# Another order for the beginning of a fused attention and feed-forward kernel: loads, norms and weight conversion

## The chip, the cores and the metric

The kernel runs on one core of one Trainium2 chip. The metric is the device time of one execution in microseconds (us).

Names used below: PE is TensorE, ACT ScalarE, DVE VectorE, POOL GpSimd, SPq the queue of SyncE that issues the loads and stores. A "values product" is PE's product of one pair's exponentials with its v (line L501 in the profiles). "Half clock" is a granted PE clock of 0.50 in the profile, as a share of full speed.

## The reference

```python
q, k, v: (8, 12, 448, 64) float32            # batch, heads, sequence, head size
q_n, k_n = rmsnorm(q) * g_q, rmsnorm(k) * g_k
attn = softmax(q_n @ k_n.T / 8) ; x = attn @ v   # then (B, H, S, D) -> (3584, 768)
xn = rmsnorm(x) * rms_g
out = (silu(xn @ w_gate) * (xn @ w_val)) @ w_out # weights are float64
```

The weights come as float64; the kernel converts them to float32 itself.

## The kernel before: what the change touches

Attention goes in 48 groups of two heads ("pairs", counted from 0). In iteration `g` PE computes the scores of pair `g`, transposes pair `g + 1` and multiplies pair `g - 1` with its values. The program fixes the order of instructions on each engine by itself; `pe(...)` emits PE's work and whatever other engines' work is due after it.

The norm of a pair is a chain over four engines: squares on ACT, sums on DVE, a power and a product on POOL, then PE's transposes, and copies to `qkT` by ACT and DVE:

```python
def squares(g, i):                       # i = 0: q, 1: k
    nc.scalar.activation(sq, st["qk", g][:, i], ACT.Square)
    after(1, reduce)                     # DVE, sums -> ms
    ...                                  # then POOL: rms_qk (power -0.5), norm_q -> qn
```

The conversion of weights is a pipeline that moves by one turn per `convert()`. Every engine has a part of it:

```python
def convert():
    ...
    if 0 <= n - 4 < len(pieces):         # POOL: add the two halves, block n - 4 is done
        ...
        nc.gpsimd.tensor_tensor(data(key).bitcast(I32), top, lo, ALU.add)
    if 0 <= n - 3 < len(pieces):         # DVE: join, three instructions
        st["cv", n - 3] = join(*st.pop(("cv", n - 3)))
    if 0 <= n - 2 < len(pieces):         # ACT: split, two instructions
        st["cv", n - 2] = split(st.pop(("raw", n - 2)))
    if n < len(pieces):                  # SPq: load of block n, into one of 6 buffers
        st["raw", n] = load_raw(pieces[n][1])
    if 0 <= n - 6 < len(pieces):         # SPq: store of block n - 6
        keep(pieces[n - 6][0])
```

The beginning:

```python
squares(0, 0)
pe(idle)
squares(0, 1)
pe(lambda: turn(0, 1))
convert(); convert()
bound()                                  # gains, and a flag from three one-row instructions
squares(1, 0); squares(1, 1)
pe(lambda: turn(0, 0))
convert()
for g in range(NG + 1):
    load_pair(g + 2)
    if g <= NPAIR:                       # NPAIR = 6
        pe(lambda: score(g, (0, 1)))     # 4 products, and 4 exponentials on ACT
        squares(g + 2, 0); squares(g + 2, 1)
        if g == 0:
            pe(lambda: score(g, (2, 3)))
        convert()
        pe(lambda: turn(g + 1, 0)); pe(lambda: turn(g + 1, 1))
        if g:
            pe(lambda: values(g - 1))
        load_v(g + 2)
        convert()
        if g:
            pe(lambda: sums(g - 1)); pe(lambda: score(g, (2, 3)))
        convert()
        continue
    ...                                  # later groups, with the feed-forward part between
```

## Time and profile before

| | before |
|---|---|
| median, 3 runs | 1637.91 us (1637.1 to 1639.52) |
| profiled span | 1636.9 us |
| PE busy | 1615.2 us, 99% |
| PE's waits, first 60 us | 12.5 us |
| PE's waits, rest | 3.0 us |
| first values product starts | 25.40 us |

A timeline line reads: start, duration, engine, source line, operation, tiles written and read, shapes, number of instructions merged; in brackets the idle time ahead of it and what ended it. Where such a line merges several pipelined products its duration contains small waits, so a "busy" PE is not PE at its peak. The lines themselves stand in the prediction.

### The profile page before, as it was taken

What the parts mean: (1) busy time and instruction counts of PE and PEld (TensorE: products, weight loads), DVE (VectorE), ACT (ScalarE), POOL (GpSimd) and SP (SyncE); (2) the same over time, 40 slices, a digit from 0 to 9 for tenths busy, and PEclk for the clock granted to TensorE, in tenths of its full rate; (3) what the DMA queues carried; (4) which work ended last, traced back from release to release, by engine and by line L of the source; (5) the groups of instructions that cost most, each with busy time, mean ns of one, the idle gap of its engine ahead of it and who ended that gap; (6) DMA issues with size and microseconds to landing.
All of it is one profiled execution on the core that took longest, in us unless ns stands there. A gap on an engine that the chain in (4) does not pass through costs nothing.

```text
span 1636.9 us, 21470 instructions
## 1 busy us (share of the span) xinstructions
PE 1615.2 (99%) x7376; PEld 1142.1 (70%) x7376; DVE 862.6 (53%) x1371; ACT 499.8 (31%) x975; POOL 631.3 (39%) x569
## 2 busy tenths in 40 slices
PE   6999999999999999999999999999999999999998
PEld 3444445678855888568875688758876587969984
DVE  6988998366542476426562354624555234433431
ACT  6756563233222332223223222322232123100110
POOL 6777777334423343334433333344343322100000
PEclk9999999999999999999999999999999999999999
DMA  7757674454613866665544655466454464557652
GB/s 195 227 158 204 183 228 128 141 185 142 211 51 117 254 203 222 204 196 162 154 139 120 196 154 159 119 204 192 146 148 124 151 192 114 146 179 241 174 150 65
DMA packets 246443, 273.28 MB, mean 167 GB/s; under 512 B 66356, under 2 KB 243252, under 8 KB 246324
## 3 DMA queue, kind: packets, MB, share of 16 engines
q1 hardware_dynamic: 246004, 271.80, 55.8%
q8 instruction: 61, 1.00, 0.3%
q14 instruction: 58, 0.48, 0.1%
q10 hardware_dynamic: 320, 0.00, 0.0%
HBM read 232.40 MB, written 39.32 MB: 166 GB/s over the span
## 4 chain that ended last, share of the span: by engine, by line
PE 92%; DVE 4%; DMA 2%; ACT 1%; SPq 0%; POOL 0%; issue 0%; DVEq 0%; ACTq 0%; POOLq 0%
PE ff L793 41%; PE ff L987 18%; PE sc L476 9%; PE av L501 8%; PE ff L888 7%; PE den L512 3%; PE ff L1018 2%; PE tr L461 2%; DVE top L646 1%; DVE top L644 1%; DVE top L645 1%; DVE rd L520 1%; DMA qk<-in_k_dram 1%; ACT e L480 1%; DMA raw<-in_moe_w_out_dram 0%; DMA raw<-in_moe_w_gate_dram 0%
## 5 line engine op out<-in xcount | busy, mean ns | idle before, releaser
L793 PE MATMUL ff<-x,w 128*128 128x224 f32 x2016 | 405.7, 353 | 0.0
L793 PEld LDWEIGHTS ff<-x,w 128*128 128x128 f32 x2016 | 378.5, 190 | 12.0 <-issue 6.6
L793 PE MATMUL ff<-xs,w 128*128 128x224 f32 x1512 | 308.0, 353 | 0.0
L793 PEld LDWEIGHTS ff<-xs,w 128*128 128x128 f32 x1512 | 283.4, 190 | 5.3 <-issue 5.3
L480 ACT ACTIVATE e<-sc,rs 112x448 f32<-112x448 f32 x384 | 212.0, 635 | 194.4 <-PE sc L476 189.3
L486 POOL TENSOR_TENSOR es<-e 112x448 f32<-112x448 f32 x82 | 95.1, 1181 | 455.9 <-ACT e L480 455.9
L490 POOL TENSOR_TENSOR es<-es,e 112x448 f32<-112x448 f32 x164 | 187.2, 1152 | 85.3 <-ACT e L480 78.8
L520 DVE RECIPROCAL rd<-rd 128x448 f32<-128x448 f32 x41 | 121.1, 2952 | 143.2 <-ACT rd L519 143.2
L987 PE MATMUL ff<-w,h 128*128 128x384 f32 x576 | 191.1, 487 | 0.0
L476 PE MATMUL sc<-qkT 64*112 64x448 f32 x768 | 179.0, 571 | 5.1 <-ACT qkT L464 5.1
L987 PEld LDWEIGHTS ff<-w,h 128*128 128x128 f32 x576 | 108.1, 190 | 75.5 <-issue 4.0
L501 PE MATMUL av<-e,vt 112*64 112x448 f32 x768 | 154.9, 545 | 0.0
L444 POOL TENSOR_TENSOR rs<-ms,mhalf 112x16 f32<-112x16 f32 (+1 forms) x50 | 143.4, 2867 | 4.2
L476 PEld LDWEIGHTS sc<-qkT 64*112 64x112 f32 x768 | 69.4, 174 | 98.0 <-issue 70.6
L501 PEld LDWEIGHTS av<-e,vt 112*64 112x64 f32 x768 | 50.8, 136 | 95.3 <-issue 75.2
L1018 PE MATMUL ff<-x,w 128*128 128x448 f32 x288 | 112.0, 542 | 0.0
L888 PE MATMUL ff<-w,h 128*128 128x384 f32 x336 | 111.0, 488 | 0.0
L987 PE MATMUL ff<-w,so 128*128 128x384 f32 x324 | 108.6, 488 | 2.0 <-DVE y L948 2.0
L805 DVE TENSOR_TENSOR cc<-ff,u 128x448 f32<-128x448 f32 x84 | 52.4, 624 | 90.4 <-PE ff L793 90.0
L888 PEld LDWEIGHTS ff<-w,h 128*128 128x128 f32 x336 | 62.8, 190 | 43.7 <-issue 2.7
L987 PEld LDWEIGHTS ff<-w,so 128*128 128x128 f32 x324 | 60.5, 190 | 44.7 <-DVE y L948 3.9
L1018 PEld LDWEIGHTS ff<-x,w 128*128 128x128 f32 x288 | 53.3, 190 | 50.8 <-issue 48.8
(86 smaller groups left out, 1470.5 us busy)
## 6 DMA issues: line engine op xcount, KB each, us to landing
w<-kept SPq DMA_DIRECT2D x552, 192.0 KB, 3.3
w<-kept_o SPq DMA_DIRECT2D x318, 192.0 KB, 3.0
kept<-w SPq DMA_DIRECT2D x96, 192.0 KB, 3.8
qk<-in_q_dram SPq DMA_DIRECT2D x48, 224.0 KB, 3.4
qk<-in_k_dram SPq DMA_DIRECT2D x96, 112.0 KB, 3.9
vt<-in_v_dram SPq DMA_DIRECT2D x48, 224.0 KB, 2.8
raw<-in_moe_w_gate_dram SPq DMA_DIRECT2D x24, 384.0 KB, 4.4
raw<-in_moe_w_val_dram SPq DMA_DIRECT2D x24, 384.0 KB, 4.7
```

The lines of the kernel that those rows point to most:

```text
L444: nc.gpsimd.tensor_tensor(st["rs", g][:, cols], ms, mhalf[0:P, cols], ALU.pow)
L476: nc.tensor.matmul(ps[0:P, 0:S], lhsT=qkT[r, 1, c * P:(c + 1) * P], rhs=qkT[r, 0, :], start=True, stop=True)
L480: nc.scalar.activation(e, ps[0:P, 0:S], ACT.Exp, scale=rs[:, n:n + 1])
L486: nc.gpsimd.tensor_tensor(es, st["e", g, 0, j], st["e", g, 1, j], ALU.add)
L490: nc.gpsimd.tensor_tensor(es, es, st["e", g, c, j], ALU.add)
L501: nc.tensor.matmul(av[j * D:(j + 1) * D, 0:S], lhsT=vt[:, j, c, :], rhs=st["e", g, c, j], start=(c == 0), stop=(c == NT - 1))
L520: nc.vector.reciprocal(rd, rd)
L793: nc.tensor.matmul(bank[:, w * HT:(w + 1) * HT], lhsT=wt[:, c * 128:(c + 1) * 128], rhs=x[:, c, :], start=onto is None and w == c == 0, st ...
L805: nc.vector.tensor_tensor(add[name], ps[:, 0:S], add[other], ALU.add)
L888: nc.tensor.matmul(ps, lhsT=st["h", b, fc][:, i * 128:(i + 1) * 128], rhs=data(("wo", b, *block_of(n, fc))), start=(fc == 0), stop=(fc == ...
L987: nc.tensor.matmul(ps, lhsT=a, rhs=data(("wo", b, name, c)), start=first and c == 0, stop=c == NFP - 1, skip_group_check=True)
L1018: nc.tensor.matmul(bank[w][:, 0:S], lhsT=data(key)[:, c * 128:(c + 1) * 128], rhs=st["x", 0, half][:, c, :], start=half == c == 0, stop=ha ...
```

## The change

The intent: PE idles and runs cold in the first 25 us because the third pair's q and k are loaded behind weights, and weight conversion and a flag stand in front of the work that PE needs. So load and square that pair first, convert weights later (the same number of turns by the end of the third group), compute the flag later, and keep PE warm with products of the identity until data come.

```diff
+    load_pair(2)
     for g in range(2):
         load_v(g)
...
     squares(0, 0)
+    warm(9)
     pe(idle)
     squares(0, 1)
     pe(lambda: turn(0, 1))
-    convert()
-    convert()
-    bound()
+    gains()
     squares(1, 0)
     squares(1, 1)
+    warm(3)
     pe(lambda: turn(0, 0))
-    convert()
+    squares(2, 0)
+    squares(2, 1)
     for g in range(NG + 1):
         b, hp = divmod(g, NPAIR)
-        load_pair(g + 2)
+        if g:
+            load_pair(g + 2)
+        if g == 0:
+            pe(lambda: score(0, (0, 1)))
+            pe(lambda: score(0, (2, 3)))
+            for i in range(2):
+                pe(lambda: turn(1, i))
+            load_v(2)
+            for _ in range(4):
+                convert()
+            load_rows()
+            continue
         if g <= NPAIR:
...
             convert()
+            if g <= 2:
+                convert()
+            if g == 2:
+                bound()
             continue
```

`warm(n)` issues n products of the 128x128 identity with itself into a bank that nobody reads. `gains()` and `load_rows()` are parts of what stood in `bound()` and ahead of it.

More of the change, by code (lines that the diff above doesn't have):

```diff
@@ L1099, in safe_scores, with gains, load_rows, bound @@
         nc.scalar.dma_start(out=gk[rows, :], in_=g_k.rearrange("(p o) -> p o", o=1))
+    load_pair(2)
     for g in range(2):
         load_v(g)
+    gqk = const.tile([128, 1], F32, name="gqk")
     rg = const.tile([128, NDC], F32, name="rg")
-    nc.sync.dma_start(out=rg, in_=moe_rms_g.rearrange("(c p) -> p c", p=128))
     row = const.tile([1, 2, D], F32, name="row")
-    nc.sync.dma_start(out=row[:, 0, :], in_=g_q.rearrange("(o d) -> o d", o=1))
-    nc.sync.dma_start(out=row[:, 1, :], in_=g_k.rearrange("(o d) -> o d", o=1))
-    gqk = const.tile([128, 1], F32, name="gqk")
-    def bound():
+    def gains():
         nc.vector.scalar_tensor_tensor(gqk, gq, 1.0 / D**0.5, gk, ALU.mult, ALU.mult)
         nc.vector.tensor_scalar(gqk, gqk, SAFE / D, -SAFE / D, ALU.min, ALU.max)
+    def load_rows():
+        nc.sync.dma_start(out=rg, in_=moe_rms_g.rearrange("(c p) -> p c", p=128))
+        nc.sync.dma_start(out=row[:, 0, :], in_=g_q.rearrange("(o d) -> o d", o=1))
+        nc.sync.dma_start(out=row[:, 1, :], in_=g_k.rearrange("(o d) -> o d", o=1))
+    def bound():
         nc.vector.tensor_tensor(row[:, 0, :], row[:, 0, :], row[:, 1, :], ALU.mult)
@@ L1116, in bound, with warm @@
         nc.vector.tensor_scalar(flag, top, 8.0, SAFE, ALU.mult, ALU.is_gt)
+    def warm(n):
+        ps = ps_m.tile([128, 512], F32, name="warm", tag="m")
+        for _ in range(n):
+            nc.tensor.matmul(ps[:, 0:128], lhsT=ident, rhs=ident, start=True, stop=True)
     squares(0, 0)
+    warm(9)
     pe(idle)
@@ L1136, in safe_scores @@
             squares(g + 2, 1)
-            if g == 0:
-                pe(lambda: score(g, (2, 3)))
             convert()
@@ L1141, in safe_scores @@
             pe(lambda: turn(g + 1, 1))
-            if g:
-                pe(lambda: values(g - 1))
+            pe(lambda: values(g - 1))
             load_v(g + 2)
             convert()
-            if g:
-                pe(lambda: sums(g - 1))
-                pe(lambda: score(g, (2, 3)))
+            pe(lambda: sums(g - 1))
+            pe(lambda: score(g, (2, 3)))
             convert()
+            if g <= 2:
+                convert()
+            if g == 2:
+                bound()
             continue
```

## The prediction

> **What bounds the kernel now.** I read the page first, then the waits of PE, then the timeline and busy times of the first 30 us, then the order of VectorE (DVE) for the 70 us after that. The page's busy table:
>
> ```profile
> PE 1615.2 (99%) x7376; PEld 1142.1 (70%) x7376; DVE 862.6 (53%) x1371; ACT 499.8 (31%) x975; POOL 631.3 (39%) x569
> ```
>
> PE is busy for 99% of the 1636.9 us span, so only work taken off PE, or time in which PE is not running dense, can matter. The waits of PE in the first 60 us:
>
> ```profile
> PE tr L461 <- POOL ms L441: 5.5, 1, 5.5
> PE sc L476 <- ACT qkT L464: 5.1, 2, 4.4
> PE tr L461 <- POOL qn L448: 1.9, 1, 1.9
> ```
>
> They sum to 12.5 us; after that the same view shows no wait up to 130 us, and 3.0 us in all from there to the end. So the change can only move the moment at which PE becomes dense. The timeline of the first 26 us (start, duration, engine, line, tiles; the bracket is idle time and its releaser), with cuts:
>
> ```profile
> 10.15 5.74 PE L476 MATMUL sc<-qkT 64*112 64x448 f32 x16 [0.72 <-ACT qkT L464]
> ...
> 12.23 2.44 ACT L480 ACTIVATE e<-sc,rs 112x448 f32<-112x448 f32 x4
> ...
> 15.85 0.63 ACT L424 ACTIVATE sq<-qk 112x512 f32<-112x512 f32 x1 [1.18 <-DMA qk<-in_q_dram]
> ...
> 16.99 0.63 ACT L424 ACTIVATE sq<-qk 112x512 f32<-112x512 f32 x1 [0.51 <-DMA qk<-in_k_dram]
> ...
> 17.53 2.19 ACT L480 ACTIVATE e<-sc,rs 112x448 f32<-112x448 f32 x4
> ...
> 18.43 0.24 POOL L441 TENSOR_SCALAR ms<-ms 112x16 f32<-112x16 f32 x1 [2.29 <-DVE ms L427]
> ...
> 18.76 3.00 POOL L444 TENSOR_TENSOR rs<-ms,mhalf 112x16 f32<-112x16 f32 x1
> ...
> 20.47 0.64 ACT L464 ACTIVATE qkT<-tr,gqk 128x448 f32<-128x448 f32 x1
> ...
> 21.16 2.82 PE L476 MATMUL sc<-qkT 64*112 64x448 f32 x8 [4.35 <-ACT qkT L464]
> ...
> 21.84 1.04 POOL L448 TENSOR_TENSOR qn<-qk,rs 112x512 f32<-112x512 f32 x1
> ...
> 25.40 3.23 PE L501 MATMUL av<-e,vt 112*64 112x448 f32 x16
> ```
>
> The reader is to see one string of ACT instructions: the third pair's squares wait for its q and k (15.85, 16.99), because those loads were issued behind three weight blocks of 384 KB; behind the squares, in order, stand the second four exponentials (17.53), one split of weights (19.59) and the copy of the second pair (20.47). So PE idles 4.35 us and starts the second pair's scores at 21.16. The first values product, at 25.40, is where the dense part begins. The busy times of each engine in 2 us stretches (the last three columns are PE's granted clock, DMA share, GB/s) show a second loss:
>
> ```profile
> 20.00:22.00 2.00, 0.84 (x4) 0.50 (x6) 1.79 (x5) 2.00 (x6) 1.92 (x2) 0.93 0.89 157
> 22.00:24.00 2.00, 2.00 (x7) 0.41 (x4) 1.96 (x2) 1.93 (x5) 2.00 (x3) 0.50 0.01 3
> 24.00:26.00 2.00, 2.00 (x12) 1.60 (x14) 2.00 (x2) 1.99 (x4) 2.00 (x3) 0.71 0.22 50
> ```
>
> After that pause PE runs at half clock until about 25.2.
>
> **What the Trainium skill says.** "TensorE: Matmul & The Clock Gate", Part 1, gives half clock after an idle window of about 3.4 us, and full clock after about as long a busy one. This trace agrees: 4.35 us idle, then 0.50. The clock column itself reads 1.00 from time 0, but the four transposes at 8.42 took 1.01 us against 0.60 at 15.82, so PE also starts cold and the column does not show it. The same page, on queue depths, calls ACT and DVE strict FIFO; the exponentials that stand behind squares waiting for data agree. "GPSIMD Engine Reference", section 1, says that GpSimd shares its SBUF interfaces with VectorE. The same VectorE instruction (L645) takes 0.36 us at 46.92 and 1.07 us at 48.18, beside one of GpSimd's weight additions (48.01 to 49.03), which agrees.
>
> **The change part by part.** The compiled order, kernel against kernel, shows everything alike from the third group on; before that:
>
> (a) *Third pair's loads first.* [...] The load at 5.39 (v before) waits for the first pair's k; in the changed kernel that place is the third pair's q. With issue times of this trace (about 0.55 us each) its q is issued at 5.4 and its two k at 5.9 and 6.5. Loads of these kinds take 2.8 to 4.8 us to land here, so all is there at about 10.3 instead of 16.9 us.
>
> (b) *Scalars later.* The gain vector no longer shares a block with three one-row instructions that wait for a load (1.23 us at 9.79). So the second pair's sums leave DVE at about 8.6 to 10.0 instead of 10.35 to 11.6, and GpSimd's wait of 0.73 us at 11.11 falls away.
>
> (c) *GpSimd's chain, which I take as the new limit.* GpSimd is busy without a pause from 8.45. After the first pair's k factors end at 10.37 it needs, with durations and gaps of this trace: 0.36 + 1.64 (second pair's q factors), 0.08 + 1.04 (its normalised q, ends 13.5), 0.35 + 1.64 (its k factors, ends 15.5), 0.35 + 3.0 (third pair's factors, ends 18.9), 0.1 + 1.04. The third pair's q is ready at 20.0, against 22.88 before; the 2.9 us won are 0.7 of the second pair and 2.2 of waiting for the sums.
>
> (d) *ACT.* First copy ends at about 10.1 or, with a warm PE, 9.7; third pair's squares end at about 11.1 (two by 0.63, the second waiting for k); eight exponentials by 0.55 end at about 15.7; second pair's copy at 16.4. No split stands between. PE starts the second pair's scores at about 16.5 instead of 21.16, and at full clock needs about 2.1 us, to 18.6. It then waits for (c) until 20.0. This slack of 1.4 us is why I take (c), not (d), as the bound.
>
> (e) *Warm products.* Twelve identity products, 24 records of PE. From the first four cold transposes I estimate about 0.4 us each: nine run from 1.3, when the identity is ready, to about 5.1, and k is there at 5.4. They cost nothing and bring the clock up. The gaps left in PE (1 us before the second pair's scores, 1.4 before the third pair's transposes) are below 3.4 us, so I expect no half clock. Transposes of the third pair (0.92 us warm, by the chain at 35.87) then end at 20.95, and the first values product starts at 21.0.
>
> **Gain: 25.4 - 21.0 = 4.4 us.**
>
> (f) *Conversion.* The number of turns is the same by the end of the third group (12), but 4 instead of 6 in the first, and 4 instead of 3 in each of the next two. PE does none of this, but DVE does three instructions per turn, 1.27 us bare and up to 1.9 beside GpSimd. Timeline of DVE from 42 us:
>
> ```profile
> 43.00 2.96 DVE L516 RECIPROCAL rd<-den 128x448 f32<-128x448 f32 x1 [1.04 <-PE den L512]
> ...
> 54.38 2.96 DVE L516 RECIPROCAL rd<-den 128x448 f32<-128x448 f32 x1 [0.70 <-PE den L512]
> ...
> 65.73 2.95 DVE L516 RECIPROCAL rd<-den 128x448 f32<-128x448 f32 x1
> ...
> 77.01 2.95 DVE L516 RECIPROCAL rd<-den 128x448 f32<-128x448 f32 x1
> ```
>
> DVE has 1.04 and 0.70 us left in groups 2 and 3, then none: it repeats every 11.3 us, just as PE does. Between the first and third reciprocal the changed kernel puts 8 turns where there were 6, and the three row instructions (0.5 us). That is 2.5 to 3.8 + 0.5 - 1.74 = 1.3 to 2.6 us of lag. What PE allows: sums end at 65.57, the next values product, which needs the bank that DVE empties, starts at 70.72; reciprocal and product take 3.6, so 1.5 us of lag are free. GpSimd's chain, likewise, ends 0.65 us before PE's transposes at 69.74. **Given back: 0 to 1.1 us; I take 0.4.**
>
> Net 4.0 us: 1637.9 - 4.0 = **1633.9 us**.
>
> **The rivals.** *DVE or GpSimd becomes the bound in groups 3 to 6*: for it speaks the repeat of 11.3 us with no idle; against it that the lag is once only and that ACT still orders DVE. If both slacks are used up, 1.5 to 2 us come back: 1636. *The third pair's k lands late* (it shares the DMA engines with the second pair's k and three loads of v), and now holds all eight exponentials: each us beyond 1.4 late costs one; landing at 13 would give about 1635. For it speaks that small k packets landed after 6 us when behind weights; against it that nothing of weights is ahead now. *Half clock returns* because PE is only partly busy from 16 to 20: up to 1.7 us lost. *Nothing gained*: a start hidden behind something else; against it, PE shows no other wait. *More than I say*: if GpSimd's steps go faster, the ACT string sets 18.6, and 1.4 us more are won, 1632.5.
>
> **Range and chances.** The start is worth 3 to 5.5 us, the give-back 0 to 2, and the three runs before spread over 2.4 us, so the median may be off by about 1. Hence 1631.8 to 1636.4. Two per cent is 33 us, more than the whole beginning: faster 0.005, slower 0.005, same 0.99.
>
> **What would show it.** Right: first values product near 21.0; PE's waits in 60 us under about 9 us (first data, one near 1, one near 1.4); third pair's squares near 10 without much waiting; granted clock 1.00 from 10 to 30 us; the transposes at 8.4 near 0.6 us; PE waits from 30 to 100 us below 1 us. Wrong: new waits of values on DVE's product, or of transposes on GpSimd, between 45 and 100 us; a clock of 0.50 near 20 us; ACT waiting for k beyond 12 us; or the dense part starting 4 us earlier with the end unmoved, which would mean a later stage had slack I do not see.

## The result, and the profile after

| | before | changed |
|---|---|---|
| median, 6 runs each, same chip | 1638.61 us (1637.07 to 1639.56) | 1641.66 us (1640.49 to 1644.73) |
| profiled span | 1636.9 us | 1639.3 us |
| PE's waits, first 130 us | 12.5 us | 11.1 us |
| first values product starts / lasts | 25.40 / 3.23 us | 21.21 / 4.92 us |
| fourth values product starts | 59.34 us | 61.41 us |

The ratio is 1.0022, with a 95% interval of 1.0009 to 1.0035. A ratio is the mean time of one kernel's fast runs over that of the other's from the same rounds, so it is not quite the ratio of the medians. The change makes the kernel slower by about 3 us, where I had said faster by 4. Both are far below 2%, so as a class it is "same", as I had expected.

The beginning went as planned. This is the timeline of the changed kernel, the same moments as shown of the kernel before:

```profile
9.94 1.14 ACT L424 ACTIVATE sq<-qk 112x512 f32<-112x512 f32 x2
...
11.20 4.30 ACT L480 ACTIVATE e<-sc,rs 112x448 f32<-112x448 f32 x8
...
16.18 1.76 PE L476 MATMUL sc<-qkT 64*112 64x448 f32 x8 [0.81 <-DVE qkT L466]
16.22 2.90 POOL L444 TENSOR_TENSOR rs<-ms,mhalf 112x16 f32<-112x16 f32 x1
...
19.20 1.04 POOL L448 TENSOR_TENSOR qn<-qk,rs 112x512 f32<-112x512 f32 x1
...
20.29 0.60 PE L461 MATMUL tr<-ident,qn 112*128 112x112 f32 x4 [2.35 <-POOL qn L448]
...
21.21 4.92 PE L501 MATMUL av<-e,vt 112*64 112x448 f32 x16
```

The squares of the third pair no longer wait, all eight exponentials run in one block, POOL's chain ends at 20.24, and the first values product starts 4.19 us earlier than before (25.40 - 21.21). But it lasts 4.92 us instead of 3.23. The busy times by stretch of the changed kernel say why (the third column from the right is PE's granted clock):

```profile
20.00:22.00 2.00, 1.71 (x12) 1.22 (x14) 1.56 (x3) 2.00 (x5) 1.40 (x3) 0.89 0.04 9
22.00:24.00 2.00, 2.00 (x8) 0.55 (x6) 1.44 (x4) 1.23 (x3) 1.92 (x2) 0.50 0.00 0
24.00:26.00 2.00, 2.00 (x12) 0.73 (x10) 0.00 (x0) 0.00 (x0) 1.92 (x2) 0.75 0.00 0
```

PE again runs at half clock, after a pause of only 2.35 us. That takes 1.69 us (4.92 - 3.23) of the 4.19 back. What is left, 2.5 us, is lost 30 us later. The timeline of the changed kernel from 39 to 62 us, all engines, cut to what matters:

```profile
39.54 2.90 POOL L444 TENSOR_TENSOR rs<-ms,mhalf 112x16 f32<-112x16 f32 x1
...
43.52 2.14 POOL L682 TENSOR_TENSOR w<-top,raw 128x384 int32<-128x384 int32 x2
...
44.57 0.37 SPq L629 DMA_DIRECT2D raw<-in_moe_w_val_dram  x1
...
45.52 0.42 SPq L397 DMA_DIRECT2D qk<-in_q_dram  x1
...
45.53 3.23 PE L501 MATMUL av<-e,vt 112*64 112x448 f32 x16
45.99 1.24 SPq L400 DMA_DIRECT2D qk<-in_k_dram  x2
...
49.59 0.63 ACT L424 ACTIVATE sq<-qk 112x512 f32<-112x512 f32 x1 [1.87 <-DMA qk<-in_q_dram]
...
51.92 0.63 ACT L424 ACTIVATE sq<-qk 112x512 f32<-112x512 f32 x1 [1.70 <-DMA qk<-in_k_dram]
...
55.21 2.18 ACT L480 ACTIVATE e<-sc,rs 112x448 f32<-112x448 f32 x4
...
55.87 3.62 PE L476 MATMUL sc<-qkT 64*112 64x448 f32 x8 [2.41 <-ACT e L480]
...
60.49 0.60 PE L461 MATMUL tr<-ident,qn 112*128 112x112 f32 x4 [1.01 <-POOL qn L448]
...
61.41 3.23 PE L501 MATMUL av<-e,vt 112*64 112x448 f32 x16
```

Read it from the bottom. Two values products follow one another here after 15.88 us (61.41 - 45.53), where the kernel before takes 11.31 in every group: 4.57 us lost. PE waited for a bank (a part of its output memory) that exponentials had to empty (55.87), then for POOL (60.49), and between them ran at half clock again (granted clock 0.50 from 56 to 58 us), so that four scores, eight records of PE, took 3.62 us. In a group without waits eight scores take 4.30 us and the first four of them 1.76, so about 1.1 us of the loss is half clock; with the two waits, 2.41 and 1.01 us, that is the 4.57 to within 0.1. The exponentials stood on ACT behind the squares of pair 5, which waited for that pair's q and k (49.59 and 51.92). These were asked for only at 45.52, because the weight load ahead of them in the queue (44.57) had itself waited since 39.98; it went out just after the first of POOL's two additions at 43.52 must have ended (one takes about 1.0 us). In the kernel before the same q was asked for at 42.53 and squared at 48.97 without a wait, although PE was 2.5 us later there (values product of the same group at 48.03):

```profile
36.69 1.01 POOL L682 TENSOR_TENSOR w<-top,raw 128x384 int32<-128x384 int32 x1 [1.38 <-ACT e L480]
...
40.54 2.90 POOL L444 TENSOR_TENSOR rs<-ms,mhalf 112x16 f32<-112x16 f32 x1
...
42.53 0.48 SPq L397 DMA_DIRECT2D qk<-in_q_dram  x1
...
48.97 1.18 ACT L424 ACTIVATE sq<-qk 112x512 f32<-112x512 f32 x2
```

The order of POOL's work shows what the change did. Before, the addition of block 5 (36.69) stood ahead of the norm chain of pair 4 (40.54); now it stands behind it (first of the two at 43.52, behind the chain at 39.54). Block 5 is added in the tenth turn. Before, nine turns were done by the end of group 1, so that it was the first turn of group 2. Now eight are done by then, because turns of the first group were put off to the ends of groups 1 and 2; the tenth is the second turn of group 2, and the norm chain comes ahead of it. The buffer that this addition frees is the one that the load of block 11, in the last turn of group 2, needs, and the loads of pair 5 come right after.

Summed to this point, from the two profiles: -4.19 + 1.69 + 4.57 = +2.07 us, and indeed the fourth values product starts at 61.41 instead of 59.34. At the end it is +2.4.

### The profile page after: what moved, and what is told of

Its sections match the earlier page's. It is cut to its first block, busy times and chain, and to the rows that moved or that the text cites. A ratio compares the mean times of both kernels' runs of the same rounds, so it can differ in the third digit from the quotient of the medians.

```text
span 1639.3 us, 21517 instructions
## 1 busy us (share of the span) xinstructions
PE 1618.7 (99%) x7400; PEld 1145.6 (70%) x7400; DVE 859.9 (52%) x1371; ACT 499.7 (30%) x975; POOL 630.7 (38%) x569
## 4 chain that ended last, share of the span: by engine, by line
PE 90%; DVE 5%; DMA 2%; POOL 1%; ACT 1%; issue 0%; SPq 0%; ACTq 0%; POOLq 0%; DVEq 0%
PE ff L793 41%; PE ff L987 18%; PE sc L476 8%; PE av L501 8%; PE ff L888 7%; PE den L512 3%; PE ff L1018 2%; PE tr L461 2%; DVE top L646 1%; DVE top L645 1%; DVE top L644 1%; POOL rs L444 1%; DVE rd L520 1%; DMA raw<-in_moe_w_gate_dram 1%; DMA raw<-in_moe_w_val_dram 1%; DMA raw<-in_moe_w_out_dram 0%
## 5 line engine op out<-in xcount | busy, mean ns | idle before, releaser
L793 PEld LDWEIGHTS ff<-x,w 128*128 128x128 f32 x2016 | 378.5, 190 | 12.0 <-issue 7.3
L682 POOL TENSOR_TENSOR w<-top,raw 128x384 int32<-128x384 int32 x72 | 78.1, 1097 | 30.2 <-DVE top L646 8.7
```

The lines of the kernel that those rows point to most:

```text
L793: nc.tensor.matmul(bank[:, w * HT:(w + 1) * HT], lhsT=wt[:, c * 128:(c + 1) * 128], rhs=x[:, c, :], start=onto is None and w == c == 0, st ...
```

## The experiments

All times are medians with 3 to 5 rounds beside the kernel before, which had 1638.02 us in the first four runs (1637.45 to 1639.25) and 1638.05 in the last four (1634.52 to 1640.54). The changed kernel's 1641.66 comes from an earlier batch, next to a before of 1638.61; so the distance to before is the safer measure.

### Asking for one pair earlier

```diff
-        if g:
+        if g not in (0, 3):
             load_pair(g + 2)
+        if g == 2:
+            load_pair(5)
```

> One load moved: the changed kernel, with the sixth pair's q and k (pair 5, counted from 0) asked for one group earlier, right behind pair 4's. Theory (a queue held up): in the changed kernel pair 5's loads stand behind a weight load that waits for GpSimd to free its buffer (44.57 us), so they land at 49.6 and 51.9, the squares and the exponentials behind them wait on ScalarE, and PE loses about 4.6 us between 45.5 and 61.4. Then this kernel has no wait of scores on exponentials near 55 us, PE takes about 11.3 us from the values at 45.5 to the next, and about 3.7 us come back (up to 0.8 stays for VectorE): about 1638.0 us where the changed kernel had 1641.7, so even with the kernel before. Rival (VectorE's additional conversion work is itself the limit, as I had foreseen it): the wait stays, in about the same size, and the time stays near 1641.7.

Measured: 1636.74 us (1636.31 to 1638.17), ratio to before 0.9993 (0.998 to 1.0007), span of the profile 1634.5. PE's waits in the first 135 us are, in all:

```profile
PE tr L461 <- POOL qn L448: 3.1, 3, 1.6
PE sc L476 <- ACT qkT L464: 1.6, 2, 0.9
PE warm L1127 <- POOL mhalf L1093: 1.4, 1, 1.4
```

The wait of scores on exponentials is gone, and pair 5's squares ran at 45.62 without a wait, by the move of one pair's three loads and nothing else: all turns of conversion stand where the change put them. The values product of pair 3 starts 11.95 us after that of pair 2 (55.52 - 43.57). So 0.64 us of the loss is left, of which 0.47 is a wait of transposes on POOL: that is the kind of lag that I had foreseen, in about the size that I had given it. The rest of the 4.57, 3.93 us, was the queue (with the half clock that followed the wait). The median fell by more than I had expected (1638.0). A part of this is not the load's: in this profile the half clock came earlier, from about 10.7 to 14.1 us (the first scores took 5.03 us instead of 4.36), and the first values product took 3.23 us, not 4.92.

### Without the doubled turns

```diff
             convert()
-            if g <= 2:
-                convert()
             if g == 2:
                 bound()
```

> The changed kernel without the two additional conversion turns at the end of groups 1 and 2 (they come later, when asked for). Both theories expect the loss of 4.6 us in groups 3 and 4 to go: the queue theory because each weight load then waits for an addition issued well before the next chain of norms on GpSimd, the VectorE theory because 2.5 us of its work go. Values products then 11.3 us apart, about 1637.0 us, 1.5 to 2 better than before. It tells whether the doubled turns are the cause at all: if they are not, the time stays near 1641.7. A third possibility: the two missing turns are made up in a burst when the feed-forward part begins near 107 us and cost 1 to 3 us there; then no gain over the changed kernel or little, with waits of PE after 100 us.

Measured: 1636.52 us (1635.01 to 1636.91), ratio 0.9987 (0.9973 to 1.0001), profile span 1635.0. Values products at 45.23 and 56.55 us, 11.32 apart, no wait left there. Pair 5's q is asked for at 39.74 here, ahead of the weight load that waits for POOL and goes out at 42.29. So the doubled turns are the cause, and, with the run before, the queue is the way by which most of the loss comes. The half clock is still there in this profile, with the same pause of 2.35 us ahead of it: the first values product takes 4.92 us. PE waits for nothing near 107 us, so no burst of turns cost time there. As the start is alike in both, this is also the cleanest comparison with the changed kernel: its fourth values product starts 4.86 us earlier (56.55 against 61.41), 0.30 of it from an earlier start.

### Identity products in the pause

```diff
             convert()
+            if g == 1:
+                warm(8)
             pe(lambda: turn(g + 1, 0))
```

> The changed kernel with eight more products of the identity between the second pair's first scores and the third pair's transposes, where PE idles from 17.9 to 20.3 us. Theory: the pause of 2.35 us, not the 3.4 us that I took as the threshold, brings PE to half clock from about 21.5 to 25.2, and the first values product takes 4.92 instead of 3.23 us. Then the granted clock stays 1.00 through 20 to 28 us, the first values product takes 3.2 us, the first sums begin near 24.3 instead of 25.96, and the time falls by 1.0 to 1.7 us to about 1640.3, if the later loss stays as it is. Rival (half clock has another cause, such as the sparse scores before): the clock still falls and values still take 4.9 us; time 1641.7.

Measured: 1640.57 us (1640.27 to 1641.65), ratio 1.0015 (1.0001 to 1.0029). The clock stays at 1.00 in every stretch from 16 to 28 us and the first values product takes 3.23 us, as expected. But this does not show that the filler did it. In this profile the half clock came earlier, from about 8.8 to 15.6 us; the first scores took 6.24 us instead of the changed kernel's 4.36, and the scores ahead of the filler ended at 19.46 instead of 17.94. Without the filler PE would have paused only 0.87 us, until POOL's data were ready at 20.33, and after pauses of 0.85 to 1.62 us in this place no half clock followed in other runs. Whether the filler keeps the clock up is thus not tested. The later loss is still there; its line on the timeline:

```profile
54.75 3.17 PE L476 MATMUL sc<-qkT 64*112 64x448 f32 x8 [2.06 <-ACT e L480]
```

So the half clock near 21 us and the late loads are two separate losses: here the first is absent and the second stays. In time the filler gains little: in this run the first values product started at 22.14 instead of 21.21. The transposes behind it started at 21.27, while POOL had their data ready at 20.33: eight products were about 0.9 us too many.

### Without identity products

```diff
-    warm(9)
...
-    warm(3)
```

> The changed kernel without its twelve products of the identity. My step (c) says that GpSimd's chain of norms sets when the third pair is ready, so a cold PE costs nothing at the end: the first transposes take 1.0 us instead of 0.6, the first scores run at half pace, yet the third pair's transposes stay at 20.3 us and the time at 1641.7 within 0.5. Rival: cold scores delay the exponentials, the second pair's copy, and by it everything: third pair's transposes at 21 to 22, time 1642.5 to 1643.5.

Measured: 1639.78 us (1639.52 to 1642.08), ratio 1.0012 (0.9999 to 1.0026): no slower than with the products. The beginning in this kernel:

```profile
20.35 0.60 PE L461 MATMUL tr<-ident,qn 112*128 112x112 f32 x4 [1.13 <-POOL qn L448]
21.27 3.23 PE L501 MATMUL av<-e,vt 112*64 112x448 f32 x16
```

The transposes start at 20.35 (20.29 with the products): POOL's chain sets this, not a cold PE. The first scores are slower (5.40 us instead of 4.36), so the pause ahead of the transposes shrinks to 1.13 us, and no half clock follows. In these two profiles the identity products thus brought the half clock rather than kept it off: they made PE finish early and wait longer. Two profiles do not show that this is so in each execution. The late loads cost here too (wait of scores on exponentials 1.63 us), and after them PE ran at half clock from about 54.1 to 64.4 us.

### The flag later

```diff
-            if g == 2:
+            if g == 5:
                 bound()
```

> The changed kernel with the three row instructions (and so the load of their flag on the queue) at the end of group 5 instead of group 2. Rival: the chain of the changed kernel goes through the flag's load at 49.8 us, where the queue stands 1.4 us for VectorE; if that holds back the loads that PE then misses, the wait of scores near 55 us goes and the time falls by 2 us or more. My theory: the pair that PE misses was asked for at 45.5 to 47.2, before the flag, behind a weight load that waited for GpSimd; so the wait of scores on exponentials stays at 1.6 to 2.4 us and the time within 1 us of the changed kernel's 1641.7 (VectorE gains 0.5 us, no more).

Measured: 1640.49 us (1639.86 to 1642.63), ratio 1.0017 (1.0 to 1.0034). The wait stays:

```profile
53.55 3.40 PE L476 MATMUL sc<-qkT 64*112 64x448 f32 x8 [1.98 <-ACT e L480]
```

The profile's chain of the changed kernel leads through the load of the flag, but moving the flag changes nothing. This run also shows that the half clock moves: up to 40 us it has the changed kernel's instructions, but the clock fell to 0.50 from about 10.7 to 14.1 us, over the first scores (5.03 us instead of 4.36). So the second pair's scores ended later, the pause was 1.62 us, the clock stayed at 1.00 from 16 to 28 us, and the first values product took 3.23 us.

### The loads alone

The kernel before, with the one line `load_pair(2)` ahead of the values' loads, and no load of that pair in the loop.

> The kernel before with one thing of the change alone: the third pair's q and k asked for ahead of the values and weights. If the late load alone made the pause at 17 to 21 us, squares no longer wait at 15.9 and 17.0, and the first values product starts 1.5 us or more earlier than 25.4: time 1636 or less. If the parts need one another, the first exponentials now wait for the first weight block, whose split stands ahead of them and which now lands about 2 us later, so they start near 14 instead of 12.2 us; the first values product then stays within 1 us of 25.4 and the time within 1 us of the kernel before. I hold the second more likely.

Measured: 1638.37 us (1637.13 to 1639.08), ratio 1.0 (0.9986 to 1.0014).

```profile
14.09 0.54 ACT L638 ACTIVATE top<-raw 128x384 f32<-128x384 f32 x1 [3.89 <-DMA raw<-in_moe_w_gate_dram]
...
14.97 2.19 ACT L480 ACTIVATE e<-sc,rs 112x448 f32<-112x448 f32 x4
```

Now the split of the first weight block holds the exponentials: they start at 14.97 instead of 12.23, PE pauses 2.05 and then 1.64 us and runs at half clock from 22 to 25 us, and the first values product starts at 25.98 instead of 25.40. Here early loads were worth nothing while a split of weights stood in front of the exponentials. In the changed kernel, which has both the early loads and the later conversion, no split stands there. The later conversion without the early loads was not run.

### The parts together, without and with identity products

Pair 5 earlier and no doubled turns, both as above; in the one kernel no `warm` at all, in the other `warm(5)` in the pause beside the twelve of the change.

> The changed kernel with pair 5 asked for earlier, without the two additional turns, and without the products of the identity. What stays of the change is the order of loads, squares and conversion. Theory: the products are not needed, since GpSimd's chain sets the start and slower first scores shorten the pause before the third pair's transposes (1.1 us in the run without products, no half clock); first values at about 21.2, no half clock, values products 11.3 us apart, 1 to 1.7 us given back near 180 us where conversion is now late: about 1635.0, 3 better than before. Rival: the products are worth their place; then this is slower than the other combined kernel by more than 1 us.

> The changed kernel with pair 5 asked for earlier, without the two additional turns, and with five more identity products in the pause before the third pair's transposes. Theory: granted clock 1.00 from 10 us on, first values at 21 us and 3.2 us long, values products 11.3 us apart, no wait of PE from 30 to 130 us; 1.5 us given back near 180 us: about 1634.5, 3.5 better than before. If the half clock returns in spite of the products, 1636.

Measured: without products 1635.05 us (1633.87 to 1635.65), ratio to before 0.9981 (0.9968 to 0.9995); with them 1635.15 us (1634.35 to 1636.45), ratio 0.9983 (0.9969 to 0.9996). Both beat both kernels, by 3 us against before. The products make no difference in the medians. The beginning without them:

```profile
19.79 0.60 PE L461 MATMUL tr<-ident,qn 112*128 112x112 f32 x4 [0.85 <-POOL qn L448]
20.70 3.23 PE L501 MATMUL av<-e,vt 112*64 112x448 f32 x16
```

From there to 77 us values products come every 11.31 or 11.32 us. With the products the granted clock was not 1.00 from 10 us on, as expected, but 0.50 from about 8.8 to 15.7 us, and the first values product started at 21.70, not 21.0.

A pattern shows when all profiles are laid side by side. Each of the six kernels with the twelve early products has one spell of half clock in the first 26 us. In two (the changed kernel and the one without doubled turns) it lies over the first values product and costs 1.69 us. In the other four it lies over the first scores, which take 5.03 to 6.24 us instead of 4.36 or 4.37, and costs less: in two of them PE still waits 1.62 us for POOL behind it. The nine products at the beginning took 3.77 and 3.66 us in those two and 4.18 to 4.21 us in the four. The two kernels without products show no such spell before 50 us, but PE starts cold in them: the transposes at 8.60 and 8.24 take 1.01 us and the first scores 5.40 and 5.47.

The profile of the combined kernel without products ends at 1632.3, 4.6 below that of before: in this one execution nearly all of the early start, 4.70 us, reached the end. The other combined kernel shows where some of it can go. In its profile there is, at 180 us, in the first stretch of the feed-forward part,

```profile
180.09 0.97 PE L512 MATMUL den<-es,ones 112*64 112x448 f32 x4 [2.29 <-ACT e L480]
```

At that place before waits 0.23 us, the changed kernel 1.08, the kernel with pair 5 earlier 1.71, the one without doubled turns 1.43, the combined one without products nothing, though it waits 1.17 us of the same kind at 149.09 (before: 0.31 at 152.91). In the kernel with pair 5 earlier ACT's exponentials there stand behind splits that wait for weight blocks (2.00 and 2.50 us). So an earlier start can meet conversion that is not ready. What decides between 0 and 2.3 us was not tested.

## Why the prediction was wrong, point by point

- **The start: right.** I said 21.0 us for the first values product, set by POOL's chain ending at 20.0. It was 21.21 and 20.24. The gain is 4.19 us where I had 4.4. The run without identity products shows that POOL sets it, and the run with the loads alone that the early loads do not give it by themselves.
- **Step (e), no half clock: wrong.** "The gaps left in PE ... are below 3.4 us, so I expect no half clock." I had the second gap at 1.4 us; it was 2.35, because the second pair's scores ended at 17.94, not 18.6, and POOL at 20.24, not 20.0. The clock fell to 0.50 before 22 us and that cost 1.69 us. I had this as a rival, with "up to 1.7 us lost". It is not certain in each execution: in the runs with pauses of 1.62 us in the same place the spell had come earlier, over the first scores, and with 1.13 us (no products) it did not come. That the pause brings the half clock is argued from these profiles; the one run meant to test it did not.
- **Step (f), what later conversion costs: the term that turned the sign.** I wrote that PE does none of the conversion and then asked only what DVE and POOL have left, and took 0.4 us. For DVE and POOL that was about right: 0.64 us are left when pair 5 is asked for earlier. What I left out is that a turn also puts a load and a store on the queue, that both need POOL's addition of an older block, and that the queue is strictly in order with the next pair's q and k behind them. Measured, the term is 4.57 us, about 1.1 of it half clock behind the wait. "Everything alike from the third group on" skipped over the addition of block 5 and pair 4's norm chain, which change places in the third group (group 2); after that group it is true of the count of turns, not of who waits for whom.
- **The rivals.** "DVE or GpSimd becomes the bound" came nearest in place and time, but its mechanism was another. "The third pair's k lands late" did not happen: that pair's squares ran at 9.94. The late load was that of pair 5. "Half clock returns" came true.
- **What would show it.** I had named new waits of values or transposes between 45 and 100 us. The largest came between them in the order, as scores waiting for exponentials (2.41 us); of the named ones transposes waited for GpSimd (1.01 us). The clock of 0.50 near 20 us, also named, came.
- **The sum.** Predicted -4.4 + 0.4 = -4.0; measured by the profiles -4.19 + 1.69 + 4.57 = +2.07, and +2.4 at the end of the kernel. The medians differ by 3.05. Runs of the changed kernel span 4.2 us between them, so I leave the remaining 0.6 us unexplained.

Open: why the half clock falls in one place or another, and whether filling the pause would keep it off; why the wait near 180 us is 0 in one profile and 2.3 in another; and whether the load or the store of the turn holds the queue first, since both need the same addition and only the load's wait shows.

## What to carry to other kernels

When work is put off, look at everything it carries, not only at the engine that computes it: a put-off step that also frees a buffer delays each load that needs the buffer, and on an in-order queue everything behind that load, here through the queue and ACT to PE, some 10 us after the step. Ask of each load on the critical path which instruction must have run before it can even be issued, and put it ahead of loads that wait. Warming products are worth what the first real work waits for; here that was GpSimd, and they bought nothing: 0.1 us between the medians of the two combined kernels.

## What the Trainium skill lacked or had wrong

- "TensorE: Matmul & The Clock Gate", section "HAM oscillation", gives as rule to have no idle gap over about 3.4 us. Here half clock followed recorded pauses of 2.35 us (twice), 2.41, 2.06 and 1.98, and even of 1.64 and 1.63 where the work around them was sparse, and in two runs it fell shortly after pauses of about 1.0 and 0.7 us; it did not follow pauses of 1.62 us (twice), 1.13 or 0.85. So the length of the gap alone does not decide. Part 1 of the page does say that the window runs freely, and its section "A second HAM failure mode" tells of a clock that oscillates with frequent short idles; what share of work within a window keeps the clock up is missing.
- No page gives the cost of a power on GpSimd as a tensor operation. It sets the start of this kernel: 1.64 us for 112x8 elements and 2.90 to 3.17 us for 112x16, against 1.04 us for a product over 112x512.
